# Where a five-tap convolution sums its taps: in SBUF, or in PSUM banks that are free between two products

## The chip, the core and the metric

The kernel runs on one core of a Trainium2 chip. Five engines work side by side, each with its own queue that it takes in order: PE (TensorE, matrix products), DVE (VectorE), ACT (ScalarE), POOL (GpSimd) and SP (it only issues transfers here). SBUF is the working memory; PE writes its products to PSUM, which has eight banks of 128 partitions by 512 fp32 values. The metric is the device time of one execution in microseconds (us).

## The reference

Three layers follow each other on `B, S, DM = 4, 768, 384`: a linear attention with decay (8 heads of 48), a gated layer with a product over the sequence, and a second gated layer, whose gate is the convolution that is changed here:

```python
xp = np.concatenate([np.zeros((B, K - 1, D)), x], axis=1)
gate_pre = np.zeros((B, S, D))
for k in range(K):                       # K = 5 taps
    gate_pre += conv_w[k][None, None, :] * xp[:, k:k + S, :]
gate = 1.0 / (1.0 + np.exp(-gate_pre))
val = x @ w_val
return (gate * val @ w_out)
```

`x` is here the output of the first gated layer, `x + gated @ w_out1`.

## The kernel before, in words

The four batches are worked one after the other. While PE does the two gated layers of batch b, the attention of batch b+1 is threaded in between, in small steps ("T" in a table of words), with its transposes (`xT`, line 478) and the first product of its gated layer (`hv`, line 499). A gated layer works on half a batch, 384 rows, with the 384 features as three blocks (f = 0, 1, 2) of 128 partitions. The steps of a half, by the words of the tables `ORDER0`, `ORDER` and `LAST`:

- `u`, `s`: products of 9 and 18 matmuls into one of two rotating PSUM tiles `d` (names `ups`, `vps`, line 522). ACT takes `ups` out as `ut` (line 535), DVE takes `vps` out as `gt` (line 562). POOL multiplies them (line 573), ACT and DVE split the result into a high and a low part `gl` (lines 575 and 576).
- `w0` to `w3`: products with the first w_out, four times nine matmuls (line 586), summed in three PSUM banks with the tags c0, c1, c2, one for each f. After the last, DVE adds them to `x2` (line 597), and ACT and POOL split that into `x2hl` (lines 598 and 599).
- `c`: the convolution of the half, function `conv`, once for each f. ACT writes the last tap (line 612), DVE adds the other four, each reading `x2` at another offset (line 615), and ACT takes the tanh (line 617). The tile is `cv`, in SBUF. There are 8 halves, so 24 convolutions and 96 instructions on line 615.
- `v`: `val`, nine matmuls; DVE multiplies it by the gate, in place on the `cv` tile (line 628), ACT and DVE split that into `ml` (lines 630 and 631).
- `o`: products with the second w_out (line 641), into the same three banks c0, c1, c2; ACT takes them out, and SP sends them off.

A PSUM or SBUF tile with a tag is handed on when its last reader is done: the next user waits for that. The scheduler orders each engine's queue by priorities (the table `LEAD`) and by its own estimate of when things are ready. PE, DVE, ACT and POOL then run their queues in that order whatever happens on the chip.

In `ORDER0` and `ORDER`, which serve batches 0 to 2, the `o` steps of a half come between its convolution and the next `w`. In `LAST`, batch 3, `w10` and `w11` of the second half follow `c0` of the first half with no `o` between them.

Of the kernel before, what the change touches and what calls it, by code (L numbers as in the profile page):

```python
# [15 lines left out]
F32 = mybir.dt.float32  # L16
F32R = mybir.dt.float32r
I32 = mybir.dt.int32
AF = mybir.ActivationFunctionType
# [11 lines left out]
HALF = 384  # L31
# [21 lines left out]
def tile_kernel(ctx, tc, pk, sv_, rk_, v_, u_, misc_, w_in, w_sgT, b_sg, w_o1, w_val,  # L53
                cw, w_o2, ident_, out):
    nc = tc.nc
    pe, act, dve, pool, sp = nc.tensor, nc.scalar, nc.vector, nc.gpsimd, nc.sync
# [4 lines left out]
    rvg = ctx.enter_context(tc.tile_pool(name="rvg", bufs=3))  # L61
    rgt = ctx.enter_context(tc.tile_pool(name="rgt", bufs=2))
    rcv = ctx.enter_context(tc.tile_pool(name="rcv", bufs=3))
# [4 lines left out]
    psC = ctx.enter_context(tc.tile_pool(name="psC", bufs=1, space=bass.MemoryType.PSUM))  # L68
# [50 lines left out]
    @contextmanager  # L119
    def lead(kind):  # L120
        at = tc.cur_priority
        tc.cur_priority = at - LEAD.get(kind, 0)
        yield
        tc.cur_priority += LEAD.get(kind, 0)
# [400 lines left out]
    ut, gt, gl, x2t, x2hl, acc, acc2, ml, gate = ({} for _ in range(9))  # L525
# [77 lines left out]
                    dve.tensor_copy(halo, x2[:, :, HALF:HALF + TAPS - 1])  # L603

    def conv(b, hf, f):
        x2 = x2t[b, hf]
        with lead("cv"):
            if b == B - 1 and hf == 1:
                t = rvg.tile([128, 512], F32, tag="vg", name="cv")[:, 0:HALF]
            else:  # L610
                t = rcv.tile([128, HALF], F32, tag="cv", name="cv")
            act.activation(out=t, in_=x2[:, f, TAPS - 1:], func=AF.Copy,  # L612
                           scale=cw_col[:, f, TAPS - 1:TAPS])
            for k in range(TAPS - 1):
                dve.scalar_tensor_tensor(out=t, in0=x2[:, f, k:k + HALF], scalar=cw_col[:, f, k:k + 1],  # L615
                                         in1=t, op0=ALU.mult, op1=ALU.add)
            act.activation(out=t, in_=t, func=AF.Tanh, scale=0.5)
        gate[b, hf, f] = t

    def val_step(b, hf, g):  # L620
        hl = x2hl[b, hf]
# [45 lines left out]
    def phase(b):  # L667
        nx = b + 1 < B
        gen = attention(b + 1) if nx else None
        wgen = rest_of_weights() if b == 0 else iter(())  # L670
        own = {"u": u_step, "s": vs_step, "w": wo_step, "v": val_step, "o": out_step}
        for word in (ORDER0 if b == 0 else LAST if b == B - 1 else ORDER).split():
            kind, at = word[0], [int(x) for x in word[1:]]
            if kind in own:
                own[kind](b, *at)
                for _ in range(2):
                    next(wgen, None)
            elif kind == "i":
                x2_init(b, *at)
            elif kind == "c":  # L680
                for f in range(KD):
                    conv(b, at[0], f)
            elif nx:
                if kind == "T":
                    next(gen)
                elif kind == "n":
                    u_step(b + 1, 0, *at)
                else:
                    {"x": xT, "h": hv}[kind](b + 1, *at)
# [146 lines left out]
```

## Time and profile before

| | us |
|---|---|
| median of 3 runs | 578.29 (574.72 to 580.51) |
| the profiled execution | 577.62 |
| its span, from first to last instruction | 575.9 |
| PE busy, share of the span | 526.2 (91%) |
| DVE | 436.1 (76%) |
| ACT | 296.0 (51%) |
| POOL | 275.9 (48%) |

Busy means that an instruction of the program was running; an engine that waits in its queue is not busy. The share is a mean over the whole program. Row groups below give it for the stretches in which the convolutions run.

### The profile page before, as it was taken

How to read it: one execution, taken by the hardware profiler on the slowest of the kernel's cores; microseconds unless marked ns; L12 is line 12 of the kernel's file. 1: busy time of each engine (PE TensorE's matmuls, PEld its weight loads, DVE VectorE, ACT ScalarE, POOL GpSimd, SP SyncE). 2: the span in 40 equal slices, each digit the busy share in tenths (PEclk: the TensorE clock that was granted, in tenths of full speed). 3: DMA queues.
4: the chain of work that ended last, by engine and by line, in shares of the span. 5: the costliest groups of instructions: out<-in, count | busy, mean ns of one | idle time of the engine just before them, and what ended most of it. 6: DMA issues, size and time to landing. Idle time of an engine off the chain costs nothing.

```text
span 575.9 us, 10711 instructions
## 1 busy us (share of the span) xinstructions
PE 526.2 (91%) x4060; PEld 451.1 (78%) x4060; DVE 436.1 (76%) x823; ACT 296.0 (51%) x695; POOL 275.9 (48%) x282
## 2 busy tenths in 40 slices
PE   8978788969989995998998998999989998999996
PEld 4756556859878984787987887888978887999985
DVE  7999999899697679955399769985398449523674
ACT  4676756645655744742366554654365635422234
POOL 7568845665834345762154226672154124722530
PEclk9688777989999997998998999999999999999999
DMA  8951513524215252232105340142113100100002
GB/s 310 384 208 42 193 30 97 166 67 139 70 42 152 88 159 72 84 127 93 42 8 173 111 152 15 60 162 83 42 25 115 56 16 0 42 1 0 1 0 83
DMA packets 27074, 53.42 MB, mean 93 GB/s; under 512 B 3088, under 2 KB 17168, under 8 KB 27024
## 3 DMA queue, kind: packets, MB, share of 16 engines
q1 hardware_dynamic: 27024, 52.75, 28.3%
q8 instruction: 32, 0.52, 0.4%
q14 instruction: 18, 0.15, 0.1%
HBM read 48.02 MB, written 4.72 MB: 92 GB/s over the span
## 4 chain that ended last, share of the span: by engine, by line
PE 47%; DVE 34%; DMA 9%; issue 4%; ACT 3%; POOL 2%; SPq 1%; POOLq 0%; DVEq 0%; ACTq 0%
PE vps L522 12%; DVE cv L615 10%; PE c L586 6%; PE ups L522 5%; PE a L372 5%; PE o L641 5%; PE hv L499 4%; PE val L522 3%; DVE SD L353 3%; DVE F L271 2%; PE a L303 2%; PE a L328 2%; DMA pk<-in_pk_dram 2%; DMA rk<-in_rk_dram 2%; DVE x L597 1%
## 5 line engine op out<-in xcount | busy, mean ns | idle before, releaser
L522 PE MATMUL vps<-wsg,vnt 128*128 128x384 f32 x576 | 112.3, 339 | 0.0
L522 PEld LDWEIGHTS vps<-wsg,vnt 128*128 128x128 f32 x576 | 100.1, 188 | 1.5
L573 POOL TENSOR_TENSOR gt<-gt,ut 128x384 f32<-128x384 f32 x32 | 35.8, 1118 | 100.4 <-DVE gt L562 76.6
L615 DVE SCALAR_TENSOR_TENSOR cv<-x,cw_col,cv 128x384 f32<-128x384 f32 x96 | 77.6, 842 | 0.2 <-ACT cv L612 0.2
L499 PE MATMUL hv<-win,x 128*128 128x512 f32 x216 | 66.9, 438 | 5.4 <-DVE cv L628 2.7
L586 PE MATMUL c<-gl,late 128*128 128x384 f32 x288 | 63.0, 345 | 1.1 <-DVE gl L576 0.7
L522 PE MATMUL ups<-x,win 128*128 128x384 f32 x288 | 60.8, 354 | 2.2 <-DVE gt L562 2.2
L358 ACT ACTIVATE SE<-SD 64x192 f32<-64x192 f32 x80 | 44.9, 561 | 23.8 <-DVE SD L353 14.7
L522 PEld LDWEIGHTS ups<-x,win 128*128 128x128 f32 x288 | 52.0, 195 | 3.8 <-DVE gt L562 2.5
L499 PEld LDWEIGHTS hv<-win,x 128*128 128x128 f32 x216 | 42.2, 205 | 14.5 <-DVE cv L628 2.9
L586 PEld LDWEIGHTS c<-gl,late 128*128 128x128 f32 x288 | 49.7, 188 | 4.3 <-ACT gl L575 1.1
L280 POOL TENSOR_TENSOR L<-pk,E 128x256 f32<-128x256 f32 x38 | 31.4, 825 | 39.9 <-PE a L372 36.3
L353 DVE TENSOR_TENSOR_SCAN SD<-SD,SD 128x288 f32<-128x288 f32 x48 | 43.7, 911 | 6.5 <-ACT SD L347 6.3
L522 PE MATMUL val<-x2hl,late 128*128 128x384 f32 x216 | 44.2, 346 | 3.7 <-DVE gt L562 2.5
L316 ACT ACTIVATE vcd<-v 64x192 f32<-64x192 f32 x84 | 30.1, 359 | 30.1 <-PE a L328 29.4
L641 PE MATMUL o<-late,ml 128*128 128x384 f32 x216 | 44.3, 343 | 1.1 <-DVE ml L631 1.1
L575 ACT ACTIVATE gl<-gt 128x384 fp32r<-128x384 f32 x32 | 16.7, 523 | 52.4 <-POOL gt L573 52.2
L522 PEld LDWEIGHTS val<-x2hl,late 128*128 128x128 f32 x216 | 37.6, 190 | 6.6 <-issue 3.1
L515 POOL TENSOR_TENSOR vnt<-vg,vnt 128x512 fp32r<-128x512 f32 x24 | 34.2, 1427 | 15.6 <-ACT vnt L514 15.5
L372 PE MATMUL a<-SE,L 128*64 128x96 f32 x304 | 33.2, 277 | 8.9 <-DVE y L377 7.4
L576 DVE TENSOR_TENSOR gl<-gt,gl 128x384 fp32r<-128x384 f32 x32 | 19.5, 611 | 28.7 <-ACT gl L575 28.7
L271 DVE TENSOR_TENSOR_SCAN F<-pk,D1F 128x260 f32<-128x260 f32 x40 | 32.4, 810 | 10.4 <-DMA pk<-in_pk_dram 7.4
(151 smaller groups left out, 1108.0 us busy)
## 6 DMA issues: line engine op xcount, KB each, us to landing
pk<-in_pk_dram SPq DMA_DIRECT2D x40, 386.5 KB, 3.6
sv<-in_sv_dram SPq DMA_DIRECT2D x39, 192.0 KB, 2.5
v<-in_v_dram SPq DMA_DIRECT2D x12, 384.0 KB, 3.7
out_dram<-ot SPq DMA_DIRECT2D x24, 192.0 KB, 1.9
rk<-in_rk_dram SPq DMA_DIRECT2D x12, 384.0 KB, 3.1
bits<-in_w_in_dram SPq DMA_DIRECT2D x6, 512.0 KB, 6.8
room_l<-in_pk_dram SPq DMA_DIRECT2D x7, 386.5 KB, 6.3
bits<-in_w_o_dram SPq DMA_DIRECT2D x7, 384.0 KB, 4.8
```

Of the source, the lines that this page charges most:

```text
L271: dve.tensor_tensor_scan(out=F[:, NW:0:-1], data0=w[:, NW:0:-1], data1=D1F[:, NW:0:-1], initial=0.0, op0=ALU.mult, op1=ALU.add)
L280: pool.tensor_tensor(out=ch(L[:, 0, :]), in0=ch(r), in1=e3[:, :, 0:C], op=ALU.mult)
L353: dve.tensor_tensor_scan(out=SD1, data0=SD1, data1=SD0, initial=0.0, op0=ALU.add, op1=ALU.mult)
L358: act.activation(out=S[half[hh], :, hh, :], func=AF.Copy, in_=d1[half[hh], :, 1:NC + 1].rearrange("p e c -> p c e"))
L372: pe.matmul(out=o, lhsT=L[:, i, c * C:(c + 1) * C], rhs=rhs[:, c], start=(i == 0), stop=(i == 1))
L499: pe.matmul(out=ps, lhsT=x[:, a, kk, j * 128:(j + 1) * 128], rhs=win[:, w, kk, DV:2 * DV], start=(z == 0), stop=(z == nmm - 1))
L515: pool.tensor_tensor(out=vnt[b][:, 1, i, :], in0=vg, in1=hi.bitcast(F32), op=ALU.subtract)]
L522: pe.matmul(out=ps, lhsT=lhs(a, kk), rhs=rhs(w, kk), start=(z == 0), stop=(z == nk * 3 - 1))
L573: pool.tensor_tensor(out=t, in0=t, in1=ut.pop((b, hf, d)), op=ALU.mult)
L586: pe.matmul(out=acc[0][f], lhsT=late["wo1"][:, a, d, f * 128:(f + 1) * 128], rhs=g[:, w, :], start=(d == 0 and q == 0), stop=(d == KV - 1 ...
L615: dve.scalar_tensor_tensor(out=t, in0=x2[:, f, k:k + HALF], scalar=cw_col[:, f, k:k + 1], in1=t, op0=ALU.mult, op1=ALU.add)
L641: pe.matmul(out=acc2[0][j], lhsT=m[:, a, j * 128:(j + 1) * 128], rhs=late["wo2"][:, w, g, :], start=(g == 0 and q == 0), stop=(g == KD - 1 ...
```

## The change

The taps are summed in a PSUM tile `cvp` with the tag c0, c1 or c2, the bank whose w_out sum has just been added to `x2`. ACT writes the last tap there, the four DVE instructions read and write it there, and the tanh moves the result to the SBUF tile `cv`. In the last half of the last batch both stay one tile in SBUF, as before. The rows of the changed kernel have other line numbers from here on: 612 becomes 615, 615 becomes 618, 617 becomes 620, 628 becomes 631, 641 becomes 644.

```diff
     def conv(b, hf, f):
         x2 = x2t[b, hf]
         with lead("cv"):
             if b == B - 1 and hf == 1:
-                t = rvg.tile([128, 512], F32, tag="vg", name="cv")[:, 0:HALF]
+                t = s = rvg.tile([128, 512], F32, tag="vg", name="cv")[:, 0:HALF]
             else:
-                t = rcv.tile([128, HALF], F32, tag="cv", name="cv")
+                s = rcv.tile([128, HALF], F32, tag="cv", name="cv")
+                t = psC.tile([128, HALF], F32, tag=f"c{f}", name="cvp")
             act.activation(out=t, in_=x2[:, f, TAPS - 1:], func=AF.Copy,
                            scale=cw_col[:, f, TAPS - 1:TAPS])
             for k in range(TAPS - 1):
                 dve.scalar_tensor_tensor(out=t, in0=x2[:, f, k:k + HALF], scalar=cw_col[:, f, k:k + 1],
                                          in1=t, op0=ALU.mult, op1=ALU.add)
-            act.activation(out=t, in_=t, func=AF.Tanh, scale=0.5)
-        gate[b, hf, f] = t
+            act.activation(out=s, in_=t, func=AF.Tanh, scale=0.5)
+        gate[b, hf, f] = s
```

Up to the first convolution each queue stands as before. From there the scheduler, which sees another tile, sets the queues in another order at many places. Two of them:

DVE's queue at the convolution of batch 0, second half. `cv` and `cvp` rows are the taps, the `L482` row takes a transpose of the next batch out of PSUM. Before:

```order
L597 TENSOR_TENSOR x_1707<-c_2195,x_1707 128x384
L615 SCALAR_TENSOR_TENSOR cv<-x_1707,cw_col,cv 128x384 x4
L229 TENSOR_TENSOR rk_120<-rk_120,u_bc 128x384
L615 SCALAR_TENSOR_TENSOR cv<-x_1707,cw_col,cv 128x384 x2
L511 TENSOR_SCALAR vg<-vg,mv,rstd 128x512
L283 TENSOR_TENSOR kh_106<-pk_99,F_108 128x256
L505 BN_STATS bs<-vg 128x6
L615 SCALAR_TENSOR_TENSOR cv<-x_1707,cw_col,cv 128x384
L482 TENSOR_TENSOR x<-a_2395,x 128x3x128
```

The same place in the changed kernel:

```order
L597 TENSOR_TENSOR x_1707<-c_2198,x_1707 128x384
L507 BN_AGGR mv<-bs 128x2
L618 SCALAR_TENSOR_TENSOR cvp<-x_1707,cw_col,cvp 128x384
L232 TENSOR_REDUCE rs<-rk_120 128x8
L509 TENSOR_SCALAR rstd<-mv 128x1
L618 SCALAR_TENSOR_TENSOR cvp<-x_1707,cw_col,cvp 128x384
L482 TENSOR_TENSOR x<-a_2401,x 128x3x128
```

The first `L482` stood behind seven taps and stands behind two.

PE's queue in batch 3, behind the last `w` of the first half. The three names `c_5573` to `c_5575` are the banks c0 to c2 of the second half's `w` sums. Before:

```order
L522 MATMUL ups<-x,win 128x384 x9
L522 MATMUL vps<-wsg_1344,vnt 128x384 x18
L586 MATMUL c_5573<-gl,late 128x384
L586 MATMUL c_5574<-gl,late 128x384
L586 MATMUL c_5575<-gl,late 128x384
L586 MATMUL c_5573<-gl,late 128x384 x2
L586 MATMUL c_5574<-gl,late 128x384 x2
L586 MATMUL c_5575<-gl,late 128x384 x2
```

The same place in the changed kernel, where they are `c_5594` to `c_5596`:

```order
L522 MATMUL vps<-wsg_1344,vnt 128x384 x36
L522 MATMUL ups<-x,win 128x384 x9
L586 MATMUL c_5594<-gl,late 128x384 x4
L522 MATMUL vps<-wsg_1344,vnt 128x384 x7
L586 MATMUL c_5595<-gl,late 128x384 x4
L522 MATMUL vps<-wsg_1344,vnt 128x384 x8
L522 MATMUL val<-x2hl,late 128x384 x2
L586 MATMUL c_5594<-gl,late 128x384 x2
L586 MATMUL c_5595<-gl,late 128x384 x2
L522 MATMUL val<-x2hl,late 128x384 x2
L586 MATMUL c_5596<-gl,late 128x384 x6
```

The `w` products moved behind 18 more `vps` matmuls and nine of `ups`, and the third bank is used last.

## Rows read from the trace of the kernel before

**Rows 1.** The page's part 4: the chain that ended last, shares by line.

```profile
PE 47%; DVE 34%; DMA 9%; issue 4%; ACT 3%; POOL 2%; SPq 1%; POOLq 0%; DVEq 0%; ACTq 0%
PE vps L522 12%; DVE cv L615 10%; PE c L586 6%; PE ups L522 5%; PE a L372 5%; PE o L641 5%; PE hv L499 4%; PE val L522 3%; DVE SD L353 3%; DVE F L271 2%; PE a L303 2%; PE a L328 2%; DMA pk<-in_pk_dram 2%; DMA rk<-in_rk_dram 2%; DVE x L597 1%
```

**Rows 2.** Windows around seven convolutions: length, busy PE, PEld, DVE, ACT, POOL; PEclk.

```profile
155.00:172.00 17.00, 15.31 (x133) 13.41 (x132) 16.83 (x30) 10.54 (x28) 7.46 (x8) 1.00 0.14 36
216.00:234.00 18.00, 12.15 (x82) 8.99 (x80) 17.96 (x30) 9.10 (x21) 10.38 (x11) 0.81 0.17 57
291.00:309.00 18.00, 14.53 (x133) 12.04 (x133) 18.00 (x28) 10.81 (x26) 9.66 (x10) 0.91 0.24 81
352.00:370.00 18.00, 16.05 (x133) 12.98 (x132) 18.00 (x34) 11.51 (x28) 10.34 (x11) 1.00 0.13 45
419.00:435.00 16.00, 13.62 (x132) 11.60 (x131) 16.00 (x27) 10.26 (x26) 8.93 (x9) 1.00 0.16 42
477.00:490.00 13.00, 10.31 (x52) 8.78 (x52) 13.00 (x29) 7.13 (x15) 6.17 (x7) 1.00 0.00 0
530.00:542.00 12.00, 11.65 (x67) 11.21 (x66) 11.76 (x20) 5.33 (x13) 6.58 (x6) 1.00 0.00 1
```

**Rows 3.** The same windows, line 615 alone: length, DVE busy (instructions).

```profile
155.00:172.00 17.00, 9.81 (x12) 1.00 0.14 36
216.00:234.00 18.00, 11.15 (x12) 0.81 0.17 57
291.00:309.00 18.00, 11.38 (x12) 0.91 0.24 81
352.00:370.00 18.00, 10.50 (x12) 1.00 0.13 45
419.00:435.00 16.00, 10.55 (x12) 1.00 0.16 42
477.00:490.00 13.00, 8.22 (x12) 1.00 0.00 0
530.00:542.00 12.00, 8.44 (x12) 1.00 0.00 1
```

**Rows 4.** DVE instructions by line: durations ns min/median/max; COPY: busy us, mean ns, idle.

```profile
L615 DVE SCALAR_TENSOR_TENSOR cv<-x,cw_col,cv x96: 578/607/1595, 155.2 to 564.1; 128x384 f32<-128x384 f32 x96
L576 DVE TENSOR_TENSOR gl<-gt,gl x32: 527/558/1409, 132.9 to 550.2; 128x384 fp32r<-128x384 f32 x32
L628 DVE SCALAR_TENSOR_TENSOR cv<-cv,val x24: 516/540/556, 168.4 to 566.0; 128x384 f32<-128x384 f32 x24
L562 DVE SCALAR_TENSOR_TENSOR gt<-vps,misc,b_bc x32: 590/614/620, 128.2 to 547.8; 128x384 f32<-128x384 f32 x32
L597 DVE TENSOR_TENSOR x<-c,x x24: 525/546/558, 153.6 to 554.7; 128x384 f32<-128x384 f32 x24
L603 DVE COPY halo<-x 128x12 f32<-128x12 f32 x4 | 0.6, 144 | 0.0
```

**Rows 5.** Timeline of DVE, then POOL, from 534 us: start, length, instruction [idle before].

```profile
534.34 3.25 DVE L615 SCALAR_TENSOR_TENSOR cv<-x,cw_col,cv 128x384 f32<-128x384 f32 x6
538.27 2.32 POOL L573 TENSOR_TENSOR gt<-gt,ut 128x384 f32<-128x384 f32 x1 [4.26 <-DVE gt L562]
```

**Rows 6.** Timeline of PE, DVE and POOL between 216 and 227 us.

```profile
226.69 0.87 PE L478 MATMUL a<-ident,y 128*128 128x128 f32 x3 [4.69 <-DVE x L482]
...
216.56 3.69 DVE L615 SCALAR_TENSOR_TENSOR cv<-x,cw_col,cv 128x384 f32<-128x384 f32 x4
221.45 1.71 DVE L615 SCALAR_TENSOR_TENSOR cv<-x,cw_col,cv 128x384 f32<-128x384 f32 x2
224.48 1.59 DVE L615 SCALAR_TENSOR_TENSOR cv<-x,cw_col,cv 128x384 f32<-128x384 f32 x1
```

**Rows 7.** Timeline of PE and ACT: two products and the tanhs nearest to them.

```profile
170.66 1.22 PE L641 MATMUL o<-late,ml 128*128 128x384 f32 x6
...
171.56 0.52 ACT L617 ACTIVATE cv<-cv 128x384 f32<-128x384 f32 x1
...
534.39 1.72 PE L586 MATMUL c<-gl,late 128*128 128x384 f32 x9
...
541.05 0.92 ACT L617 ACTIVATE cv<-cv 128x384 f32<-128x384 f32 x2
```

## The prediction

> **What bounds the kernel now.** I read the chain of waits first. PE holds 47% of it and DVE 34%, and the largest single DVE entry is the convolution's line 615 with 10% [rows 1]. PE is busy 91% of the span, so over the whole program PE is the bound; but a share of the whole says nothing about a stretch, and I looked next at the seven windows in which the convolutions run that the change touches. There DVE has no room: 16.83 of 17 us, 17.96 of 18, and 18.00 of 18 in the next two [rows 2]. PE is the engine with holes: window length less PE's busy time is 1.69, 5.85, 3.47, 1.95, 2.38, 2.69 and 0.35 us, together 18.4. [...] So while a convolution runs, DVE is the bound and PE waits for results that stand in DVE's queue behind the taps. Only what shortens DVE there, and up to what PE is missing there, can shorten the program.
>
> **What a tap costs, and why.** The same instruction takes 578 ns at best, 607 in the median, and up to 1595 [rows 4]. Rows that differ in one thing tell what stretches it. Line 576 also has two tensors from SBUF, and spreads from 527 to 1409 ns. Lines 628, 562 and 597 read one of their two tensors from PSUM, in the same shape, and never exceed 556, 620 and 558 ns [rows 4]. Where POOL stands idle (4.26 us before 538.27), six taps run in 3.25 us; less the last one's own 0.607 us, that is 0.53 us from one to the next [rows 5]. And a POOL product that meets the taps behind them takes 2.32 us [rows 5]. So a DVE instruction with both tensors in SBUF and a POOL instruction hold each other up, and one that takes one of the two from PSUM does not. The changed tap reads `x2` from SBUF and its running sum from PSUM: it moves from the first kind to the second.
>
> **The sum, part by part.** Twelve undisturbed taps are 12 x 0.53 = 6.4 us. The windows show 9.81, 11.15, 11.38, 10.50, 10.55, 8.22 and 8.44 us for twelve [rows 3], 70.05 in all, so DVE gets back 3.4, 4.8, 5.0, 4.1, 4.2, 1.8 and 2.0 us: 25 us, if a tap in PSUM costs what an undisturbed one in SBUF does. The twelve taps of the last half stay as they are.
>
> No row shows DVE writing to PSUM, or a sum handed on there from one instruction to the next. Below, a gain is not excluded: line 628, the same operation with its second tensor in PSUM, has a median of 540 against 607 ns (it lacks the column of weights), so at most 67 ns less, 84 x 0.067 = 5.6 us. Above, the near row is the whole fixed part of an instruction paid once more: a copy of 12 columns takes 144 ns [rows 4], 84 x 0.144 = 12.1 us. I take nothing, because line 562, which has a column and a tensor from PSUM, has 614 against 607 ns, the nearest row to the new tap.
>
> [...]
>
> What DVE gets back is worth at most PE's hole in the same window: the smaller of the two is 1.7, 4.8, 3.5, 1.9, 2.4, 1.8 and 0.4, together 16.5 us. Not all of it lies ahead of the wait. In the second window PE's 4.69 us end with line 482 [rows 6]; seven taps stand ahead of it, 3.69 + 1.71 + 1.59 = 6.99 us instead of 7 x 0.53 = 3.7, so 3.3 of the 4.7 us go, 70%. I take 70% throughout: 11.5 us. (There the order helps too: two taps stand ahead of that row in the changed queue. Elsewhere the new order may do harm, and I count both as noise.) The clock: at the lower level 0.19 x 18 + 0.09 x 18 = 5.0 us of PE's pace are lost in two windows; both follow holes that shrink, and I take half, 2.5 us.
>
> The sums now hold the banks until the tanh. In the first window the `o` products started at 170.66 and the last tanh ended at 172.08; in batch 3 `w10` started at 534.39 and the last tanh ended at 541.97 [rows 7]. The first, 1.4 us, is covered by the 3.4 us that this convolution gets shorter. Of the second, 7.6 us, the convolution gives back 2.0, and the changed PE queue has 18 `vps` and 9 `ups` matmuls more ahead of `w10`: at 1.72/9 = 0.19 us each [rows 7] that is 5.1 us, so nothing is left for the first bank, and the third comes later still. I charge 1.5 us for this and for the order together. If that cover were gone, it would be 5.6 us. ACT's first tap and tanh change their memory but not their number, 3 + 3 in a window in which ACT is busy 10.54 of 17 us [rows 2]: nothing. POOL's instructions get shorter where they met taps; they wait for DVE more than DVE for them, and I count nothing. No transfer is added.
>
> Sum: 577.6 for the profiled execution - 11.5 - 2.5 + 1.5 = 565.1; its time is 0.7 below the median, so I predict 566 us. Its own range goes from all of the 16.5 and 5.0 (557) to the upper price in PSUM: 12.1/7 = 1.7 us less in each window leaves 13 of the 16.5, at 70% 9, and no clock gained (571).
>
> **Rivals.**
> - *Given back* (17%). Every queue is in another order from the first convolution on, and PE has 91%. If the new order opens holes as long as those that it closes, the gain shrinks to under 5.8 us (1%, about what a measurement of this kernel tells from no change): around 575. For it: holes of 1 to 2.7 us in nearly all these windows, so they come easily. Against: the gain repeats in seven places, and an order would have to be bad in most.
> - *The lock stays* (6%): a tap that still reads `x2` from SBUF meets POOL as before. Then nothing changes but the bank waits, 1.4 us and what is left of 7.6: 579. Against it stand 24 rows of line 628 that never exceed 556 ns [rows 4].
> - *PSUM is the slower place for a chain* (15%), the one that ends slower. Each tap reads what the one before has just written. Today's mean step is 70.05/84 = 0.834 us; a step in PSUM longer than that makes DVE, busy all through these windows, longer than before. At twice the 0.40 us that 384 columns take (0.53 less a fixed part of 0.13, cf. the 0.144 of 12 columns) a step is 0.93, 84 x 0.096 = 8.1 us more, and the last tanhs no longer come early, so that about 2.5 us of waiting for `w10`'s banks join: 588. For it: no such write in the trace. Against: reads from PSUM cost nothing more.
>
> **How the numbers follow.** The forecast has 62%. The range from 555 to 583 holds it nearly whole and the two middle rivals; the slower one lies outside. Faster by over 1%: 0.62; within 1%: 0.23 (the first two rivals); slower: 0.15.
>
> **What would show it.** Right: line 618 with a median near 610 and a maximum under 700 ns, no longer spread; about 6.4 us for twelve; PE's holes in the windows under 8 us together. The price in PSUM shows as the median of line 618, the lock as a maximum over 1000 ns. Wrong: taps at 610 ns and the time unchanged, which makes it the order; or PE rows of lines 586 or 644 that wait for the tanh on line 620, which makes it the banks.

## The result: 557.8 us, 20 less than before

The changed kernel takes 557.75 us (median of 4 runs, 556.39 to 561.67) against 577.48 for the kernel before on the same chip: a ratio of 0.9657, 95% interval 0.9605 to 0.9709. The forecast was 566. A ratio, here and below, is worked out from the fast runs alone, so it can differ from the quotient of the two medians by up to 0.3%. The execution profiled below took 556.39 us, with a span of 554.3.

The chain of waits of the changed kernel can't be set beside [rows 1] as it is: its page follows it back only to 195.97 us, where the chain of the kernel before goes back to the start. So here are both from the end of line 597's additions for batch 0's second half (216.6 and 214.4 us) to the end of the program, the kernel before first (shares of that stretch; the view cuts its lines off):

```profile
by line: PE vps L522 17.0%; DVE cv L615 13.5%; PE ups L522 8.2%; PE c L586 8.0%; PE o L641 6.4%; PE a L372 5.2%; PE val L522 4.4%; PE hv L499 3.9%; issue 3.5%; PE a L328 2.7%; PE a L303 2.5%; DVE x L597 2.0%; DVE SD L353 1.8%; DMA rk<-in_rk
```

```profile
by line: PE vps L522 19.5%; PE c L586 9.6%; PE ups L522 9.2%; PE o L644 6.7%; DVE cvp L618 6.7%; PE val L522 4.5%; issue 4.4%; PE a L372 4.2%; PE hv L499 3.9%; PE a L303 3.1%; PE a L328 3.0%; DVE cv L618 1.9%; PE a L297 1.8%; DVE SD L353 1.
```

The taps went from 13.5% of that stretch to 6.7% and 1.9%, together 8.6%. The DVE instructions of the changed kernel by line (durations in ns as minimum/median/maximum) answer to [rows 4], and the last row, POOL's product, to [rows 5]:

```profile
L618 DVE SCALAR_TENSOR_TENSOR cvp<-x,cw_col,cvp x84: 585/615/624, 153.4 to 519.0; 128x384 f32<-128x384 f32 x84
L618 DVE SCALAR_TENSOR_TENSOR cv<-x,cw_col,cv x12: 603/606/1377, 533.7 to 542.6; 128x384 f32<-128x384 f32 x12
L576 DVE TENSOR_TENSOR gl<-gt,gl x32: 527/559/1317, 130.4 to 528.6; 128x384 fp32r<-128x384 f32 x32
L573 POOL TENSOR_TENSOR gt<-gt,ut x32: 997/1015/1268, 126.4 to 526.9; 128x384 f32<-128x384 f32 x32
```

The 84 taps in PSUM lie within 40 ns of each other. The twelve of the last half, which stayed in SBUF, still reach 1377 ns, and line 576, which nobody touched, 1317. POOL's product, up to 2.32 us before, now ends within 1.27.

The windows of the seven convolutions in the changed kernel (length; busy PE, PEld, DVE, ACT, POOL; PEclk), for [rows 2]:

```profile
153.40:168.00 14.60, 14.60 (x133) 13.09 (x132) 14.60 (x30) 10.63 (x27) 7.43 (x9) 1.00 0.15 42
214.00:229.00 15.00, 13.02 (x122) 10.00 (x120) 15.00 (x35) 10.59 (x25) 10.06 (x11) 1.00 0.27 79
281.00:296.00 15.00, 15.00 (x148) 13.37 (x147) 14.76 (x32) 12.41 (x31) 9.61 (x11) 1.00 0.42 129
336.50:352.00 15.50, 14.33 (x124) 11.48 (x123) 15.50 (x36) 11.89 (x29) 9.43 (x11) 1.00 0.16 52
402.50:415.00 12.50, 12.48 (x132) 10.70 (x131) 12.33 (x26) 10.07 (x26) 7.99 (x9) 1.00 0.18 49
458.00:469.00 11.00, 9.72 (x50) 8.30 (x49) 11.00 (x28) 6.44 (x14) 5.21 (x7) 1.00 0.00 0
510.50:520.50 10.00, 10.00 (x59) 10.00 (x58) 9.27 (x18) 4.78 (x11) 5.48 (x6) 1.00 0.01 2
```

DVE is still nearly full, but PE has few holes left (0, 1.98, 0, 1.17, 0.02, 1.28 and 0, together 4.5 us), and the granted clock is 1.00 throughout. Line 618 alone, the first two and the sum of the same windows, for [rows 3]:

```profile
153.40:168.00 14.60, 7.05 (x12) 1.00 0.15 42
214.00:229.00 15.00, 7.14 (x12) 1.00 0.27 79
...
sum 93.60, DVE 48.74; mean DVE 6.96
```

The twelve taps of each window, added over all seven, take 48.74 us instead of 70.05: DVE got 21.3 us back. One row of DVE's timeline, four taps of the last of these windows that follow each other directly:

```profile
515.41 2.19 DVE L618 SCALAR_TENSOR_TENSOR cvp<-x,cw_col,cvp 128x384 f32<-128x384 f32 x4
```

Where did 20 us of the span go? The stretch from the end of the first three additions of line 597 to the end of the program, cut at each later set of additions, holds nearly all of it. First the kernel before, then the changed one (second piece and sum; columns as above):

```profile
216.60:291.40 74.80, 66.53 (x478) 58.01 (x477) 52.71 (x97) 34.13 (x80) 35.25 (x34) 0.93 0.24 78
...
sum 420.80, PE 392.98 PEld 347.80 DVE 297.98 ACT 202.70 POOL 173.24; mean PE 49.12 PEld 43.47 DVE 37.25 ACT 25.34 POOL 21.66
```

```profile
214.40:280.40 66.00, 61.63 (x455) 53.69 (x455) 48.57 (x97) 32.12 (x75) 32.67 (x33) 1.00 0.28 88
...
sum 400.80, PE 387.15 PEld 344.44 DVE 278.86 ACT 202.52 POOL 165.78; mean PE 48.39 PEld 43.05 DVE 34.86 ACT 25.31 POOL 20.72
```

420.8 less 400.8 is 20.0. PE's idle time, length less busy, went from 27.8 to 13.65 us: 14.2 of the 20. The other 5.8 us are PE's busy time (392.98 to 387.15) for the same matmuls. The kernel before has three stretches at the lower level of the clock between its first convolution and 575 us, 13.6 us long together; the changed kernel has none up to 551.6 us. The three stretches, and then the changed kernel (columns as above):

```profile
223.80:230.60 6.80, 3.91 (x12) 3.13 (x12) 6.80 (x13) 1.50 (x3) 2.54 (x3) 0.50 0.36 116
261.40:264.80 3.40, 3.40 (x19) 2.96 (x19) 1.84 (x5) 0.90 (x2) 0.70 (x1) 0.51 0.37 116
305.70:309.10 3.40, 3.15 (x27) 2.82 (x28) 3.40 (x8) 2.36 (x6) 0.95 (x2) 0.50 0.25 68
```

```profile
153.40:551.60 398.20, 387.25 (x2962) 344.54 (x2960) 278.96 (x562) 202.62 (x464) 165.88 (x169) 1.00 0.23 72
```

The place of the longest hole in [rows 6], now (PE and DVE; start, length, instruction [idle before]):

```profile
215.41 0.61 DVE L618 SCALAR_TENSOR_TENSOR cvp<-x,cw_col,cvp 128x384 f32<-128x384 f32 x1
215.94 0.55 DVE L482 TENSOR_TENSOR x<-a,x 128x384 fp32r<-128x384 f32 x1
...
217.32 0.49 PE L478 MATMUL a<-ident,y 128*128 128x128 f32 x3
```

Line 482 comes behind two taps, and the transposes that wait for it follow PE's other work with no idle time. That is shorter taps and a new order at once; the experiments take the two apart.

### The profile page after: what moved, and what is told of

It is laid out like the page before. It is cut to its first block, busy times and chain, and to the rows that moved or that the text cites. A ratio compares the mean times of both kernels' runs of the same rounds, so it can differ in the third digit from the quotient of the medians.

```text
span 554.3 us, 10705 instructions
## 1 busy us (share of the span) xinstructions
PE 520.3 (94%) x4060; PEld 448.4 (81%) x4060; DVE 417.0 (75%) x823; ACT 296.2 (53%) x695; POOL 267.5 (48%) x282
## 4 chain that ended last, share of the span: by engine, by line
PE 40%; DVE 16%; issue 3%; DMA 2%; POOL 1%; ACT 1%; POOLq 0%; SPq 0%; ACTq 0%; DVEq 0%
PE vps L522 12%; PE c L586 6%; PE ups L522 6%; PE o L644 4%; DVE cvp L618 4%; PE val L522 3%; PE a L372 3%; PE hv L499 2%; PE a L303 2%; PE a L328 2%; DVE cv L618 1%; PE a L297 1%; DVE SD L353 1%; DVE rk L229 1%; DMA rk<-in_rk_dram 1%
## 5 line engine op out<-in xcount | busy, mean ns | idle before, releaser
L573 POOL TENSOR_TENSOR gt<-gt,ut 128x384 f32<-128x384 f32 x32 | 33.8, 1057 | 98.7 <-DVE gt L562 80.5
L499 PE MATMUL hv<-win,x 128*128 128x512 f32 x216 | 65.2, 431 | 3.7 <-DVE cv L631 2.2
L618 DVE SCALAR_TENSOR_TENSOR cvp<-x,cw_col,cvp 128x384 f32<-128x384 f32 x84 | 48.7, 612 | 0.4 <-ACT cvp L615 0.2
L271 DVE TENSOR_TENSOR_SCAN F<-pk,D1F 128x260 f32<-128x260 f32 x40 | 35.3, 884 | 16.5 <-DMA pk<-in_pk_dram 12.3
L644 PEld LDWEIGHTS o<-late,ml 128*128 128x128 f32 x216 | 37.5, 187 | 2.4 <-DVE ml L634 1.0
```

The source lines that it names most:

```text
L271: dve.tensor_tensor_scan(out=F[:, NW:0:-1], data0=w[:, NW:0:-1], data1=D1F[:, NW:0:-1], initial=0.0, op0=ALU.mult, op1=ALU.add)
L499: pe.matmul(out=ps, lhsT=x[:, a, kk, j * 128:(j + 1) * 128], rhs=win[:, w, kk, DV:2 * DV], start=(z == 0), stop=(z == nmm - 1))
L573: pool.tensor_tensor(out=t, in0=t, in1=ut.pop((b, hf, d)), op=ALU.mult)
L644: pe.matmul(out=acc2[0][j], lhsT=m[:, a, j * 128:(j + 1) * 128], rhs=late["wo2"][:, w, g, :], start=(g == 0 and q == 0), stop=(g == KD - 1 ...
```

## The experiments

The theory: a tap that reads its running sum from PSUM no longer meets POOL, DVE gets 21 us back, and PE's holes close. Rivals: the new order of the queues does it; or it is the bank, or where a result is written. In the edits, `io` lists where the five partial sums lie (`s` in SBUF, `t` in the c bank). Ratios are against the kernel before on the same chip (577.8 us for `e1` to `e4`, 578.7 for `e5` to `e8`, 577.8 for `f1` and `f2`, 580.3 for `g1` and `g2`), with 95% intervals. Unless it is said otherwise, a run's queues are in the order that the scheduler set for that run.

That POOL is what a tap meets can be read from the traces. In the kernel before, 40 of the 96 taps overlap no POOL instruction in time, and none of these takes more than 609 ns; of the 56 that overlap one, 40 take more than 650. In the changed kernel 60 of the 84 taps in PSUM overlap a POOL instruction, and none takes more than 624.

### What of the move matters: banks, writing or reading

`e1_last_write` holds the banks but sums in SBUF; `e2_every_other` alternates.

```diff
-            act.activation(out=t, in_=x2[:, f, TAPS - 1:], ...)
+            io = (s, s, s, s, t)          # e2_every_other: (s, t, s, t, t)
+            act.activation(out=io[0], in_=x2[:, f, TAPS - 1:], ...)
...
-                dve.scalar_tensor_tensor(out=t, ..., in1=t, ...)
+                dve.scalar_tensor_tensor(out=io[k + 1], ..., in1=io[k], ...)
```

> Theory (the lock: a tap that reads both its tensors from SBUF and a POOL instruction hold each other up): all four taps here read x2 and their running sum from SBUF; only the last one writes its result to the PSUM bank, from which the tanh takes it. The bank is held as in the change, but no tap is freed. So the taps keep their spread (mean over 800 ns, maximum over 1300), the last tap of each three among them, and the time stays at that of the kernel before, 575 to 583 us. Rival (the gain came from the new order of the queues and from the tanh that reads PSUM, not from the taps): this kernel has the bank, the PSUM tanh and a new order too, so most of the 20 us should come, under 567 us.

Measured: 581.39 us, ratio 1.0069 (1.0033 to 1.0105), as the theory expected. With the banks held, another order of the queues and nothing gained by the taps, the kernel is 3.6 us slower.

> The running sum goes SBUF, PSUM, SBUF, PSUM, PSUM: of the four taps the second and the fourth read it from PSUM, the first and the third read it from SBUF and write it to PSUM. Theory (what counts is where the second tensor is read, not where the result goes): taps that read PSUM have a maximum under 650 ns, taps that read SBUF and write PSUM keep a maximum over 1100 ns; half of the disturbed taps are freed, so some 10 to 13 us of DVE time and about half of the gain, 564 to 572 us. Rival (the place of the result counts as well, or a PSUM write is what frees a tap): the three taps that write PSUM are all under 650 ns and the time is near the change, 557 to 562 us.

Measured: 572.8 us, 0.9892 (0.9857 to 0.9928), 0.8 us above what the theory expected: the gain is 5.0 us, a quarter and not half, from 8.8 us of DVE time (70.05 less 36.2, 12.6 and 12.5). The taps of this run by operands (busy us, mean ns of one | idle before; the last row has minimum/median/maximum) decide:

```profile
L619 DVE SCALAR_TENSOR_TENSOR cvp<-x,cw_col,cv 128x384 f32<-128x384 f32 x42 | 36.2, 875 | 0.2 <-ACT cv L616 0.2
L619 DVE SCALAR_TENSOR_TENSOR cvp<-x,cw_col,cvp 128x384 f32<-128x384 f32 x21 | 12.6, 605 | 0.0
L619 DVE SCALAR_TENSOR_TENSOR cv<-x,cw_col,cvp 128x384 f32<-128x384 f32 x21 | 12.5, 601 | 0.1
...
L619 DVE SCALAR_TENSOR_TENSOR cvp<-x,cw_col,cv x42: 595/792/1654, 153.1 to 534.0; 128x384 f32<-128x384 f32 x42
```

The form that reads from SBUF and writes to PSUM takes 875 ns in the mean, as long as in `e1_last_write` (873 for 75 taps in SBUF). The forms that read the sum from PSUM take 601 and 605, whichever memory they write to, and at most 615 and 618, where the form that reads from SBUF reaches 1654. So the second tensor that is read decides, and an output in PSUM alone does not help: 875 ns with it, 873 without. `e1_last_write` and `e2_every_other` also have the same order in the queues of PE, DVE, ACT and POOL, so the 8.6 us between them come from where the partial sums lie.

### Order or memory: each without the other

In `f1_psum_old_order` the changed kernel's instructions stand in the order of the kernel before on every engine, and in `f2_sbuf_new_order` the kernel before's in the order of the changed one.

```diff
     for b in range(B):
         phase(b)
 
+    queue_as_listed(tc)    # each engine's queue as in the other kernel, by ordering edges alone
```

> The changed kernel, every instruction of it, but each engine issues in the order of the kernel before. So the taps stand in PSUM and nothing else of the change is there. If the memory of the taps makes the gain: seven halves of twelve taps at about 615 ns, 7.4 us each, as in the changed kernel; the additions of a half end at about the changed kernel's distances (66, 56, 66, 55, 52, 23 us); 557 to 566 us. If the order of the queues makes it: taps at 615 ns too, but DVE's time won is lost again where PE stands for the same instruction as before (near 222 us for 4.7 us, near 285 us); 570 to 577 us. In between, 566 to 570, each has a part, read as the share of the 19.7 us.

> The kernel before, every instruction of it, with the taps in SBUF, but each engine issues in the order of the changed kernel. If the memory of the taps makes the gain, the taps stay at 600 to 2300 ns beside POOL (mean about 850) and the order alone is worth little: 572 to 580 us. If the order makes the gain: the taps are as long, but PE is fed in time; 558 to 566 us. Worse than 580 would say that the new order fits only the shorter taps.

| | order of before | order of the change |
|---|---|---|
| sum in SBUF | 577.8 | 580.07, 1.0029 (0.9993 to 1.0066) |
| sum in PSUM | 566.81, 0.9786 (0.9715 to 0.9857) | 557.75, 0.9657 (0.9605 to 0.9709) |

The order alone gains nothing in the total: 580.07 lies at the upper end of where the memory theory put it. The memory alone is worth 11 us: 566.81 lies just above that theory's range and in the band in which each has a part, though the taps are as short as in the changed kernel (587/616/624 ns). So 9 us need both.

The total of the order hides two effects. The place of the longest hole in `f1_psum_old_order`, its second piece, and the second piece of `f2_sbuf_new_order`:

```profile
219.79 0.52 PE L539 MATMUL a<-ident,y 128*128 128x128 f32 x3 [1.57 <-DVE x L543]
```

```profile
212.90:283.40 70.50, 64.97 (x479) 56.68 (x479) 48.42 (x97) 33.87 (x80) 34.17 (x34) 0.98 0.26 82
```

```profile
220.40:289.30 68.90, 63.48 (x455) 54.94 (x455) 51.47 (x97) 32.35 (x75) 33.66 (x33) 0.98 0.27 84
```

Line 539 here is line 478. With shorter taps in the old order the hole of 4.69 us is down to 1.57, and the second piece goes from 74.8 to 70.5 us; the new order brings the rest, to 66.0. With the taps in SBUF the new order shortens that piece too, to 68.9, but makes the other seven 9.2 us longer.

Most of the 9 us that need both lies in one place of `f1_psum_old_order`, where PE's `w10` products (line 647 there) stand for ScalarE's tanh (681):

```profile
516.75 0.49 ACT L681 ACTIVATE cv<-cvp 128x384 f32<-128x384 f32 x1 [1.65 <-DVE cvp L679]
517.29 0.44 PE L647 MATMUL c<-gl,late 128*128 128x384 f32 x1 [1.06 <-ACT cv L681]
...
519.36 0.47 ACT L681 ACTIVATE cv<-cvp 128x384 f32<-128x384 f32 x1
519.88 2.34 PE L647 MATMUL c<-gl,late 128*128 128x384 f32 x5 [2.15 <-ACT cv L681]
```

and the windows of that run around and behind these waits:

```profile
512.00:519.20 7.20, 4.68 (x26) 4.10 (x24) 7.17 (x15) 3.86 (x9) 4.04 (x4) 1.00 0.00 0
519.20:526.00 6.80, 6.12 (x18) 5.72 (x19) 1.29 (x4) 1.12 (x3) 3.07 (x3) 0.50 0.01 2
```

The old order sends `w10` right behind the convolution whose taps now hold its banks. PE stands 3.2 us in two waits, and from 519.2 us the granted clock is 0.50 for 6.8 us, the lower level. To test the cause, `g1_old_order_bank_a` gives that one half other banks and leaves the order alone:

```diff
-                t = psC.tile([128, HALF], F32, tag=f"c{f}", name="cvp")
+                t = (psA.tile([128, 512], F32, tag=f"a{f}", name="cvp")[:, 0:HALF] if b == B - 1 else
+                     psC.tile([128, HALF], F32, tag=f"c{f}", name="cvp"))
```

> As the run with PSUM taps in the old order (566.8 us), but the taps of the last half but one stand in banks a0 to a2. In that run TensorE stood 1.06 and 2.15 us at 517 and 520 us until ScalarE's tanh had emptied a c bank, and 6.8 us at the lower granted clock followed. If the held banks are what the old order costs there: both waits and the lowered stretch go, 3.2 + 3.4 = 6.6 us, 559 to 563 us, and the seventh distance between additions falls from 30.6 to about 24. If it is the old order as such: 566 to 568, the distance stays near 30.

Measured: 560.77 us, 0.9682 (0.9629 to 0.9735), as expected if the held banks cost it. PE waits no more there. The same pieces as above (the seventh and the sum), in `f1_psum_old_order` and then here:

```profile
512.30:542.90 30.60, 27.39 (x138) 26.10 (x137) 14.09 (x30) 8.07 (x18) 9.59 (x10) 0.89 0.00 1
...
sum 410.10, PE 392.09 PEld 347.70 DVE 274.84 ACT 202.46 POOL 163.96; mean PE 49.01 PEld 43.46 DVE 34.36 ACT 25.31 POOL 20.49
```

```profile
514.20:538.10 23.90, 23.90 (x138) 23.59 (x137) 14.12 (x29) 8.10 (x19) 9.63 (x10) 1.00 0.00 1
...
sum 403.30, PE 388.78 PEld 345.34 DVE 275.23 ACT 202.33 POOL 163.48; mean PE 48.60 PEld 43.17 DVE 34.40 ACT 25.29 POOL 20.43
```

30.6 became 23.9 us, and PE is busy in all of it. The ladder from the first additions to the end is thus 420.8 (before), 410.1 (memory), 403.3 (memory, without the bank wait), 400.8 (the change). 17.5 of the 20.0 us belong to the taps' memory once no bank is waited for, and 2.5 to the order. These are lengths of one profiled execution each; by their totals this run and the changed kernel can't be told apart, since the intervals overlap.

`e8_old_place` tried one place of the order by hand: the line 482 rows of batch 1 stay behind late taps.

```diff
+                if b == 1 and i >= 3:
+                    behind.enter_context(tc.issue_after(tapped[{3: 6, 4: 8, 5: 11}[i]].ins))
                 dve.tensor_tensor(out=x[:, 1, :, j * 128:(j + 1) * 128], ...)
```

> The change, but DVE takes the three transposes of batch 1 out of PSUM (line 482 in the change) only behind the 7th, 9th and 12th tap of batch 0's second convolution, where they stood before, not behind the 2nd, 8th and 11th. The stretch from the end of that half's additions to the end of the next half's took 74.8 us before and 66.0 in the change. Theory (the taps' length made that difference): the taps run at 0.61 us, PE's hole ahead of these transposes is 1 to 2 us and the stretch takes 67 to 69 us; the whole 558 to 561 us. Rival (the new place in the queue made it): the hole is 3 us or more, the clock falls after it, and the stretch takes 71 to 75 us; the whole 563 to 567 us.

Measured: 564.86 us, 0.9779 (0.9728 to 0.983). The total lies where the rival put it, but the second piece took 69.0 us, where the theory put it (before 74.8, the change 66.0). The rest of the queues was put in another order too, PE's transposes (line 478) wait for no transpose that DVE takes out, and the fifth piece took 59.9 instead of 55.4. So the total shows nothing about that place; `f1_psum_old_order` shows it better.

### DVE's time given back

`e5_one_more` adds a fifth instruction to each convolution of the seven halves, which adds zero times `x2`:

```diff
+            if b < B - 1 or hf == 0:
+                dve.scalar_tensor_tensor(out=t, in0=x2[:, f, 0:HALF], scalar=0.0, in1=t, ...)
```

> The change with a fifth DVE instruction of the same shape behind the four taps of each convolution in PSUM: it adds 0.0 times x2, so the sum stays. 21 more instructions of some 0.46 to 0.53 us are 10 to 11 us of DVE time in the seven windows, where DVE is still busy 98 to 100% in the change and PE 87 to 100%. Theory (what DVE loses or gains in these windows goes to the end nearly whole, as the change gained 20 us of the program from 21 us of DVE time): 566 to 569 us. Rival (with the holes closed PE is the bound there, and DVE time is worth half or less): 558 to 563 us.

Measured: 578.47 us, 0.9995 (0.9961 to 1.003). 21 instructions with a median of 550 ns, 11.6 us of DVE, cost the whole gain of 20.7 us. The direction is as expected, the size is not: it lies above both ranges, and is more than was put in. The queues stand in another order here too, so how much of the excess is order stays open.

### The last half, and one step more

In `e3_all_halves` the last half uses the c banks too, in `e4_last_in_a` the banks a0 to a2, which nobody wants any more; `e7_batch3_in_a` puts both halves of batch 3 there. `g2_last_in_a_same_order` is `e4_last_in_a` with each queue in the changed kernel's order.

```diff
-                t = s = rvg.tile([128, 512], F32, tag="vg", name="cv")[:, 0:HALF]
+                s = rvg.tile([128, 512], F32, tag="vg", name="cv")[:, 0:HALF]
+                t = psA.tile([128, 512], F32, tag=f"a{f}", name="cvp")[:, 0:HALF]   # e3: psC, c{f}
```

> The last half sums its taps in the banks c0 to c2 as well. Theory (there the banks are not free: the first half's products with the second w_out want them right then): its twelve taps go from 8.9 to about 7.3 us together, but 27 matmuls of 0.18 us (4.8 us) that ran beside the convolution now wait for its last tanh; the time is 3 to 8 us above the change, 561 to 566 us. Rival (PE finds other work, or the end hangs on DVE alone): 1 to 2 us below the change, 556 us.

Measured: 559.98 us, 0.9699 (0.965 to 0.9747), 2.2 us above the changed kernel and so between the two expectations; the last piece, 20.5 us in the changed kernel, became 24.0. PE's longest wait for the tanh there is 0.8 us, far less than the 4.8 expected.

> The last half sums its taps in the three PSUM banks a0 to a2 that the attention has left by then; all else is the change. Theory (the end of the program hangs on DVE's chain of taps): the twelve taps go from 8.9 to about 7.3 us, nobody waits for a bank, and the time is 1 to 2 us below the change, 555.5 to 557 us. Rival (PE's own work sets the end there): within 0.5 us of the change.

Measured: 555.18 us, 0.9597 (0.9557 to 0.9638); last piece 18.9.

> The changed kernel's order on every engine, the taps of the very last half too in PSUM (banks a0 to a2). If its twelve taps (8.9 us in the changed kernel, 7.4 in the other halves) are on the path: 556.2 us, 1.5 below the changed kernel, and the last distance 19.0 instead of 20.5 us. If another order made the gain of the earlier run of these banks: 557 to 558 and a last distance of 20.5.

Measured: 555.65 us, 0.9598 (0.9556 to 0.9641); last piece 18.9 us. The taps of `g2_last_in_a_same_order`:

```profile
L681 DVE SCALAR_TENSOR_TENSOR cvp<-x,cw_col,cvp x96: 580/614/624, 154.2 to 541.3; 128x384 f32<-128x384 f32 x96
```

So the very last half was left out for the sake of its banks, not of its taps. In a free bank it gives 1.6 us more, in the piece at the end in both runs; by their totals alone the intervals of these and of the changed kernel overlap. But for two neighbours in DVE's queue `e4_last_in_a` already has the changed kernel's order on PE, DVE, ACT and POOL, so the two runs say the same. Theirs are the lowest medians here.

> Both halves of batch 3 sum in a0 to a2, so that the w products of the second half need not wait for the first half's tanh. Theory (that wait is covered by the reordered PE queue already): within 1 us of the run in which only the last half does so, 554 to 556.5 us. Rival (the bank costs time there): 2 us or more below it, 553 us.

Measured: 557.38 us, 0.9625 (0.9549 to 0.97). That is 2.2 us above `e4_last_in_a`, outside what either side expected, but the intervals overlap, so it is not to be told from it; the seventh piece, where the wait would stand, takes 23.2 us, and 23.4 in the changed kernel. In the changed kernel's order the bank wait costs nothing: its trace has no wait of line 586 for the tanh; `f1_psum_old_order` shows that this is the order's doing.

`e6_ml_too` adds to `e4_last_in_a` the same for the split behind the gate: the product stays in the bank of `val`, and the split, line 637 here (634 in the changed kernel), reads it there.

```diff
-            dve.scalar_tensor_tensor(out=t, in0=t, scalar=1.0, in1=ps, op0=ALU.add, op1=ALU.mult)
+            dve.scalar_tensor_tensor(out=ps, in0=t, scalar=1.0, in1=ps, op0=ALU.add, op1=ALU.mult)
+            t = ps
```

> The last half sums in a0 to a2, and the gate's product with val stays in val's own PSUM bank, from which ACT takes the high part and DVE the low part ml: 24 more DVE instructions that no longer read both tensors from SBUF (mean 0.78 us before, 1.42 at most). Theory (each freed instruction gives DVE back what POOL held it up by): ml under 650 ns at most, 24 x 0.2 = about 5 us of DVE time, and 2 to 4 us of the program against the run that differs in ml alone, 551 to 553 us. Rival (the product holds one of the two rotating banks d for some 1.2 us longer each time, and PE waits for them): 556 to 562 us.

Measured: 573.25 us, 0.9923 (0.9889 to 0.9956). The split is freed (524/550/558 ns; in the changed kernel it reached 1600), and yet the kernel is 18 us slower than `e4_last_in_a`, above both ranges. By the edit the `d` banks, two for all of `ups`, `vps` and `val`, are held longer, and every queue is in another order; the two were not separated. PE's largest wait in that trace is for line 311 (5.6 us in three), and no `ups`, `vps` or `val` product waits for a reader of the gate's product.

## Why the prediction was right, and which terms were mis-sized

- **What bounds the kernel** held: DVE in the seven windows, PE behind it. In the old order and without the bank wait the first seven pieces lose 1.7, 2.9, 2.9, 1.2, 2.4, 1.4 and 0.4 us of PE's idle time, where the smaller of DVE's relief and PE's hole was put at 1.7, 4.8, 3.5, 1.9, 2.4, 1.8 and 0.4.
- **The mechanism** held, and `e2_every_other` narrows it to the read. The rival that the lock stays fell with the maximum of 624 ns. The size was missed: the forecast gain was some 12 us, the measured one 20, so that the time lies close to the 557 us that the prediction had as the far end of its own range.
- **The price in PSUM**, taken as nothing, is nothing: 615 against 607 ns in the median, and 605 against 601 for writing to PSUM rather than to SBUF with the same reads. The rival of a slow chain in PSUM fell. Reading from PSUM costs nothing either: with one of its two tensors from PSUM and its result to SBUF a tap of `e2_every_other` takes 601 ns, in the mean as in the median, against a median of 605 for the 40 taps of the kernel before that meet no POOL instruction.
- **DVE's relief**: 21.3 us for 25. The twelve taps take 6.7 to 7.1 us, not 6.4. A tap that follows another directly still does so after 0.525 us, in the median of 30 such pairs; the row at 515.41 us shows three of them, (2.19 - 0.62) / 3 = 0.52. But other DVE work stands between most of them, and a tap that stands alone counts its full 0.61 us. It mattered little, since PE's hole was the smaller number in five of the seven windows.
- **The share of the holes** was put too low: 70% of 16.5 us, 11.5, read off one hole and carried to all. At that hole it was right: in the old order the wait for line 482 is 1.57 us, in `g1_old_order_bank_a` 1.42, so 3.1 to 3.3 of the 4.69 went, and 3.3 were forecast. Over the whole stretch PE's idle time falls by 27.8 - (403.3 - 388.78) = 13.3 us there, since the holes of three windows closed wholly. In the changed kernel it falls by 14.2; the order adds 0.9.
- **The clock**: 2.5 us, half of what two windows lost by their granted clocks in [rows 2], 0.81 and 0.91. The trace of the kernel before has the granted clock at two levels, 1.00 and 0.50, and these windows hold the lowered stretches from 223.8 us (6.8 us) and from 305.7 us (3.3 of its 3.4 us). In the old order and without the bank wait PE's busy time falls by 392.98 - 388.78 = 4.2 us (one lowered stretch of 3.4 us, from 255.7 us, is left there), in the changed kernel by 5.8, more than the 5.0 of the two windows, since a lowered stretch outside them (from 261.4 us) went as well. In the changed kernel every lowered stretch between the first convolution and the last microseconds went.
- **Banks and order** were charged 1.5 us and gave 0.9 + 1.6 = 2.5 by the ladder above. This is the term that was furthest off, and the prediction had set the help of the order aside as noise. That the wait for the banks is covered was right: in the changed kernel's trace no product waits for the tanh, with the `vps` and `ups` matmuls moved ahead of `w10`. The old order shows the wait uncovered. It is 3.2 us, less than the 5.6 written down, but costs 410.1 - 403.3 = 6.8, because 6.8 us at a granted clock of 0.50 come on top (half of their pace, 3.4 us, by an estimate). The rival that a new order gives the gain back fell in this kernel, but `e8_old_place`, which changes nothing but order, is 7 us slower. `e5_one_more` and `e6_ml_too` lose more, with their order not separated from the rest of the edit.

The terms differ by 1.8 (holes), 1.7 (clock) and 4.0 us (banks and order), together 7.5: the 12.5 of the sum became 20.0.

## What to carry to other kernels

Where VectorE is full and GpSimd works beside it, look for VectorE instructions with two SBUF tensors and a wide spread of durations (here 578 to 1595 ns); a chain that is summed in place can stand in a PSUM bank (here 585 to 624 ns), and here it was the tensor read there that freed it (601 and 605 ns in the mean, against 875 with the result alone there). Then ask who wants that bank next and what stands ahead of it in the queue: the same edit was worth 11 or 20 us, and 6.8 of the difference hung on that. When a scheduler reorders everything behind an edit, pin each kernel to the other's order before crediting either.

## What the runs showed of the hardware beyond that

ScalarE was quicker here with one side in PSUM. The first tap and the tanh in the changed kernel, in PSUM for seven halves and in SBUF for the last:

```profile
L615 ACT ACTIVATE cvp<-x,cw_col x21: 563/567/578, 152.8 to 512.2; 128x384 f32<-128x384 f32 x21
L615 ACT ACTIVATE cv<-x,cw_col x3: 602/603/606, 532.8 to 535.1; 128x384 f32<-128x384 f32 x3
...
L620 ACT ACTIVATE cv<-cvp x21: 463/491/497, 158.3 to 519.7; 128x384 f32<-128x384 f32 x21
L620 ACT ACTIVATE cv<-cv x3: 517/525/525, 540.1 to 544.1; 128x384 f32<-128x384 f32 x3
```

36 ns less for writing there, 34 less for reading. And a short wait cost double in one place: the 3.2 us of waiting in `f1_psum_old_order` came with 6.8 us at a granted clock of 0.50, and both went together in `g1_old_order_bank_a`.
